# Third column block of an expert product: its last plain products stand among the slices of the seven products, e2 is converted later and in three parts, and the last expert's rows get four buffers

## The chip, the cores and the metric

One core of one Trainium2 chip runs the whole program as one launch. The metric is device time in microseconds (us), the median of the runs shown. One further execution was taken by the hardware profiler; all rows below are of that execution, and a time such as 953.37 is counted from the first instruction of its span.

Engines: PE is TensorE (PEld its weight loads), DVE is VectorE, ACT is ScalarE, POOL is GpSimd, and SP is the engine whose queue issues the plain DMA transfers.

## The reference: what is computed

```python
def reference(**kwargs):
    attn_out = _attn_ref(q, k, v, proj)          # 2 x 8 heads, 768 x 64, masked by hash buckets
    x = attn_out.transpose(0, 2, 1, 3).reshape(B * S, H * D)      # 1536 x 512
    x = ((x @ w1) * (x @ w2) @ w3) @ w_out                        # 512 -> 1024 -> 1024 -> 512
    p = domain_probs / (domain_probs.sum(-1, keepdims=True) + 1e-09)
    out = np.zeros((N, D), dtype=np.float32)
    for e in range(4):
        h = np.maximum(x @ e1[e], 0.0)                            # 1536 x 1024
        out += p[:, e:e + 1] * (h @ e2[e])                        # 1536 x 512
    return out
```

The change touches only the last loop, the four experts (from about 476 us to the end), and mostly `h @ e2[e]`.

## The kernel before, in words

Every float32 operand is split into a high part (made by ACT) and a low part (made by DVE, the difference), and a product is three TensorE passes: high x high, high x low, low x high.

An expert `e` has two stages. The 1536 token rows are three blocks of 512.

**Up stage** (`fp_products`, four steps `fp` = 0 to 3). `x @ e1[e]` is made by seven products instead of eight (Strassen's scheme); `CHAIN` gives their order 1, 2, 6, 5, 7, 4, 3. Each has a part M (512 columns, the first two token blocks) and a part N (256 columns, the third). N gives the third block's rows, kept in `row_y`: four rows of `xa` and two buffers `m_t`.

**Down stage.** For the first two token blocks `h @ e2[e]` is again seven products, in the order 1, 4, 6, 2, 5, 7, 3. Each is cut into four slices (`slice_mm`; slice `p.s` is product p, slice s), each of 12 matmuls of 256 columns into the banks `u_ps`: products 1, 6, 5, 3 into banks 1 and 3 (`YB2`), products 4, 2, 7 into banks 0 and 2 (`WB2`). Product 6 continues in the banks where 1 stood. For the third block the product is plain: eight pieces `y_down(e, 0)` to `y_down(e, 7)`, here O0 to O7, each 12 matmuls of 512 columns into the four banks `o_ps`. In the kernel before O0 to O3 stand in the up stage (behind product 7 of steps 1, 2, 3 and at the end of step 3), and O4 to O7 each stand ahead of one slice of product 1: O4, 1.0, O5, 1.1, O6, 1.2, O7, 1.3, then 4.0 to 4.3, 6.0 and so on.

Operands of the slices:
- Left: a slice's rows are split into one of three buffers `hl` (ACT, then DVE) just ahead of it. Products 6, 5, 7 and 3 read sums. One is made by POOL (`sums_a`); the others are made by accumulating DMA transfers that POOL issues (`added`): those of product 6 are `sums_b`'s `(s, e, 2, s)`. One may go out only when slice `4.s` has been split, since it overwrites what that slice reads.
- Right: e2 comes into `ro` (two halves of 512 columns per `fp`, `load_o`) and is split into ten units of `ring`; POOL makes four sums per `fp` out of `ro` (`t`, L897). The plain product O(2fp+h) uses unit 4h+fp and unit 8+h; units 8 and 9 are reused by each `fp`. `prep_b` writes the sums into units given by `UNITS` when the units are free.

Results: `gather` (DVE, L1065) adds each bank's half into `xa` and, for the last expert, stores it. The third block's rows go through `third` (L1205): load the rows from `out` into the one buffer `xo`, multiply and add o_ps on DVE, store them back; four times per expert, d = 0 to 3, each waiting for the store before. For expert 0 there is nothing to load.

The order on each engine is set by a planner (`emit_all`): every operation has an engine, a planned duration, dependencies and a due time (`clock[0]` counts planned PE time; Q = 2600 ns), and the planner writes the operations into each engine's in-order queue. On the chip an engine then waits at the head of its queue. The planner charges a plain DMA 700 to 800 ns on SP and 1900 ns until it has landed, and an accumulating DMA 1000 ns on POOL and 2200 ns more.

```python
LAT["SP"] = {"PE": 1900, "ACT": 1900, "DVE": 1900, "POOL": 1900, "SP": 1900, "NONE": 0}
for s in range(4):                 # down stage of an expert, before
    y_down(e, 4 + s)
    slice_mm(e, 1, s, free_)
last_o[0] = [third(e, d) for d in range(4)]
```

The functions that the diff touches, with the line numbers of the profile:

Of the kernel before, what the change touches and what calls it, by code (L numbers as in the profile page):

```python
# [85 lines left out]
def tile_lsh_attention_moe(ctx, tc, qk, v, projc, w1, w2, w3T, w_out, dp, e1, e2, out):  # L86
# [789 lines left out]
    def load_o(e, fp):  # L876
        name = ("O", e, fp)
        T = clock[0]
        for h in range(2):
# [15 lines left out]
        for m, x, y, need_ in ((1, quad_(fp, 0, 1), quad_(fp, 0, 0), []), (3, quad_(fp, 1, 1), quad_(fp, 0, 1), []),  # L895
                               (2, quad_(fp, 1, 1), quad_(fp, 0, 0), [("td", e - 1, 6, fp // 2), ("xd", 7, 0), ("xd", 7, 1)]), (4, quad_(fp, 1, 0), b_sum(2, fp), [])):
            op(("t", e, fp, m), "POOL", 700, lambda m=m, x=x, y=y: nc.gpsimd.tensor_tensor(out=b_sum(m, fp)(), in0=x(), in1=y(), op=ALU.subtract),  # L897
               [("dc", name), ("dd", name), ("dl", name, 0), ("dl", name, 1)] + need_ + [("t", e, fp, k) for k in {1: (), 3: (1,), 2: (1,), 4: (2,)}[m]], T + Q)
# [296 lines left out]
    def third(e, d):  # L1195
# [5 lines left out]
        free_ = [("st3", i - 1)] if i else []  # L1201
        T = clock[0] + 15 * Q
        if e:
            op(("l3", i), "SP", 800, lambda: nc.sync.dma_start(out=xo[0], in_=rows), free_ + [("st3", i - 4)], T - 10 * Q)
            op(("ox3", i), "DVE", 650, lambda: nc.vector.scalar_tensor_tensor(  # L1205
                out=xo[0], in0=o_ps[d], scalar=p, in1=xo[0], op0=ALU.mult, op1=ALU.add), src + [("l3", i)], T)
        else:
            op(("ox3", i), "DVE", 650, lambda: nc.vector.tensor_scalar(out=xo[0], in0=o_ps[d], scalar1=p, scalar2=None, op0=ALU.mult),
               src + free_, T)
        op(("st3", i), "SP", 800, lambda: nc.sync.dma_start(out=rows, in_=xo[0]), [("ox3", i)], T)  # L1210
# [4 lines left out]
    UNITS = {1: (0, 1, 2, 3), 4: (0, 1, 8, 9), 6: (2, 3, 0, 1), 2: (4, 5, 6, 7), 5: (8, 9, 2, 3), 7: (0, 1, 4, 5), 3: (6, 7, 8, 9)}  # L1215
# [172 lines left out]
```

## Time and profile before

| what | value |
|---|---|
| median of 3 runs | 976.85 us (975.31 to 977.16) |
| the profiled execution, its own time | 977.87 us |
| its span, first to last instruction | 976.1 us |
| PE busy | 959.2 us, 98% of the span |
| DVE, ACT, POOL busy | 729.5, 574.5, 319.2 us |
| mean granted TensorE clock | 0.997 |

The profiled execution is 1.77 us longer than its span and 1.02 us longer than the median. PE is busy nearly all the time, so what is left to win or lose lies in the places where PE's timeline shows a wait, and in how long PE's work itself takes at the granted clock.

### The profile page before, as it was taken

To read this page: it belongs to the slowest core of one execution; us is meant where nothing else is said; L and a number is where in the kernel's file an instruction comes from. 1 tells how busy PE (TensorE), PEld (TensorE's weight loads), DVE (VectorE), ACT (ScalarE), POOL (GpSimd) and SP (SyncE) were. 2 spreads that over 40 slices of the span, in tenths; PEclk is the share of its full clock that TensorE was granted. 3 is DMA by queue.
4 is the path that set the end of the run, shared out by engine and by line. 5 is a ranking of instruction groups with operands and counts; after the bars stand their busy time and mean duration, and the time that the engine had idled before them with its cause. 6 is when DMAs were issued, how large, how long until landed. Compare 5 with 4: busy or idle time off the path is not lost. (4 is left out here: it accounts for less than half of the span.)

```text
span 976.1 us, 15888 instructions
## 1 busy us (share of the span) xinstructions
PE 959.2 (98%) x5803; PEld 852.0 (87%) x5803; DVE 729.5 (75%) x1403; ACT 574.5 (59%) x1078; POOL 319.2 (33%) x372
## 2 busy tenths in 40 slices
PE   8999999999999999999999999999999999999997
PEld 6989899998888888888788899888998889988887
DVE  6999999998699965955765687556875568754477
ACT  5989989888534322444665554655546555465452
POOL 6888778876100000000102341023410234102340
PEclk9999999999999999999999999999999999999999
DMA  6755444330144421400311083110841108410074
GB/s 165 188 128 129 107 115 112 96 96 12 55 130 130 128 88 44 129 22 1 109 33 33 22 157 114 33 33 22 165 138 33 33 22 167 136 34 11 1 161 131
DMA packets 54110, 84.54 MB, mean 87 GB/s; under 512 B 7016, under 2 KB 28840, under 8 KB 54032
## 3 DMA queue, kind: packets, MB, share of 16 engines
q1 hardware_dynamic: 46976, 70.94, 24.8%
q0 software_dynamic: 6912, 12.59, 7.2%
q8 instruction: 45, 0.74, 0.3%
q14 instruction: 33, 0.27, 0.1%
q10 hardware_dynamic: 144, 0.01, 0.0%
HBM read 50.36 MB, written 6.29 MB: 58 GB/s over the span
## 5 line engine op out<-in xcount | busy, mean ns | idle before, releaser
L176 PE MATMUL u_ps<-ring,hl 128*128 128x256 f32 x1344 | 169.1, 285 | 4.5 <-DVE hl L185 3.7
L176 PEld LDWEIGHTS u_ps<-ring,hl 128*128 128x128 f32 x1344 | 165.7, 193 | 8.8 <-DVE hl L185 6.0
L897 POOL TENSOR_TENSOR ro<-ro 128x256 f32<-128x256 f32 x32 | 28.0, 875 | 279.7 <-DVE ring L185 278.4
L176 PE MATMUL u_ps<-xh,slot 128*128 128x512 f32 (+1 forms) x576 | 114.4, 355 | 0.0
L176 PEld LDWEIGHTS u_ps<-xh,slot 128*128 128x128 f32 x576 | 95.5, 189 | 16.0 <-DVE xh L185 0.4
L494 ACT ACTIVATE e<-e,sm 128x768 f32<-128x768 f32 x96 | 89.3, 932 | 8.0 <-DVE e L491 7.1
L176 PE MATMUL u_ps<-xh,slotl 128*128 128x256 f32 (+1 forms) x456 | 90.5, 346 | 1.5 <-DVE xa L1055 1.5
L176 PE MATMUL o_ps<-ring,hl 128*128 128x512 f32 x384 | 91.9, 390 | 0.0
L491 DVE TENSOR_SCALAR_CACHE_REDUCE e<-s_ps 128x768 f32<-128x768 f32 x96 | 89.9, 948 | 2.3 <-PE t_ps L539 1.4
L176 PEld LDWEIGHTS o_ps<-ring,hl 128*128 128x128 f32 x384 | 71.3, 188 | 14.4
L176 PEld LDWEIGHTS u_ps<-xh,slotl 128*128 128x128 f32 x456 | 72.7, 189 | 12.7 <-DVE xa L1055 1.9
L176 PE MATMUL u_ps<-slot,slotl 128*128 128x512 f32 (+1 forms) x384 | 72.9, 338 | 0.0
L504 POOL TENSOR_SCALAR e<-e,sm 128x768 f32<-128x768 f32 x72 | 67.2, 940 | 11.6 <-DVE sm L509 6.2
L185 DVE TENSOR_TENSOR ring<-ro,ring 128x512 fp32r<-128x512 f32 x48 | 36.5, 759 | 42.0 <-ACT ring L182 40.5
L176 PEld LDWEIGHTS u_ps<-slot,slotl 128*128 128x128 f32 x384 | 59.0, 190 | 8.0
L176 PE MATMUL pv_ps<-etx,vv 128*128 128x256 f32 x384 | 58.2, 290 | 0.1
L1047 ACT ACTIVATE hl<-gl 128x512 fp32r<-128x512 f32 x52 | 32.9, 633 | 42.1 <-PE u_ps L176 18.9
L176 PE MATMUL s_ps<-ka,hh 128*128 128x512 f32 x192 | 53.1, 358 | 2.1 <-DVE e L491 1.7
L176 PEld LDWEIGHTS pv_ps<-etx,vv 128*128 128x128 f32 x384 | 49.8, 189 | 1.9 <-DVE xa L567 0.8
L176 PE MATMUL s_ps<-kb,ll 76*128 76x512 f32 x192 | 49.8, 341 | 0.5 <-DMA kb<-bt 0.5
L1065 DVE SCALAR_TENSOR_TENSOR xa<-u_ps,prob,xa 128x256 f32<-128x256 f32 x112 | 49.4, 482 | 0.9 <-PE u_ps L176 0.9
L176 PE MATMUL u_ps<-xh,slotm 128*128 128x512 f32 x216 | 49.9, 389 | 0.0
(209 smaller groups left out, 2049.2 us busy)
## 6 DMA issues: line engine op xcount, KB each, us to landing
wraw<-in_w SPq DMA_DIRECT2D x16, 512.0 KB
wraw<-in_w3T SPq DMA_DIRECT2D x16, 512.0 KB
wraw<-in_e SPq DMA_DIRECT2D x32, 256.0 KB
ro<-in_e SPq DMA_DIRECT2D x32, 256.0 KB
r<-in_qk SPq DMA_DIRECT2D x15, 384.0 KB
gl<-gl POOLq DMA_DIRECT2D x20, 256.0 KB, 4.5
wraw<-in_w_out SPq DMA_DIRECT2D x8, 512.0 KB
out<-xo SPq DMA_DIRECT2D x16, 256.0 KB
```

Of the source, the lines that this page charges most:

```text
L176: nc.tensor.matmul(out=o, lhsT=l, rhs=r, start=start, stop=stop, skip_group_check=chained)
L185: nc.vector.tensor_tensor(out=dst, in0=ps, in1=f(hi), op=ALU.subtract)
L491: op(("mx", u, t), "DVE", 873, lambda ps=ps, m=m, e=e: nc.vector.tensor_scalar(out=cols(e), in0=row(ps), scalar1=THR, scalar2=None, op0=AL ...
L494: op(("ex", u, t), "ACT", 921, lambda e=e, m=m, rs=rs: nc.scalar.activation(out=e, in_=e, func=AF.Exp, scale=-1.0, bias=m, accum_out=rs), ...
L504: return "POOL", 872, lambda: nc.gpsimd.tensor_scalar(out=e, in0=e, scalar1=r[:, t:t + 1], scalar2=1.0, op0=ALU.mult, op1=ALU.mult)
L897: op(("t", e, fp, m), "POOL", 700, lambda m=m, x=x, y=y: nc.gpsimd.tensor_tensor(out=b_sum(m, fp)(), in0=x(), in1=y(), op=ALU.subtract), [ ...
L1047: op(("gh", n), "ACT", 600, lambda: nc.scalar.activation(out=hi(), in_=src(), func=AF.Relu if relu else AF.Copy, scale=sign), after, T)
L1065: nc.vector.scalar_tensor_tensor(out=xa[:, t, w], in0=src(), scalar=p, in1=xa[:, t, w], op0=ALU.mult, op1=ALU.add)
```

## The change: what it does

1. The plain products move: O0 behind product 7 of step 1, O1 behind product 7 and O2 behind product 3 of step 2, O3 behind product 7 of step 3; then O4 ahead of slice 1.0, O5 ahead of 1.1, O6 ahead of 1.3 and O7 ahead of 6.0 (`BEFORE`). `third` is now called after O7.
2. `load_o` converts an `fp` of e2 in three parts (a left half for each h, and both right halves, units 8 and 9, together) and begins only when PE has done the first product of that step, M part (`GATE`); for expert 0, step 0, the third product. POOL's sums follow the part that each needs.
3. The units of `ring` for products 4, 6, 5, 7 and 3 are dealt anew, so that product 4 no longer uses units 8 and 9.
4. In the last expert the four `third` rows use four buffers: the halves of `raws[0]`, `xo` and `m_t[1]` (`third_buf`), with due times earlier than before.
5. Planner's numbers: an accumulating transfer is charged 3500 ns on a lane per slice index instead of 2200; POOL's sums 840 and 1050 instead of 700; gathers 393 instead of 380; step 1 of expert 0's e1 conversion is due 3 Q later.

```diff
+    for i in range(4):
+        LAT[f"Q{i}"] = dict.fromkeys(LAT["SP"], 0)
...
     def load_u(e, fp, after, z_after):
-        T = clock[0] + (16 * Q if e and fp == 1 else 0)
+        T = clock[0] + ((16 if e else 3) * Q if fp == 1 else 0)
...
+    def GATE(e, fp):
+        return ("M", e, fp, 1 if e or fp else 3)
...
     def load_o(e, fp):
...
-            op(("dh", name, h), "ACT", 600, lambda units=units, src=src: hi_of(units(0), src()),
-               [("dl", name, h)] + unit_free[u] + unit_free[v], T)
-            op(key, "DVE", 620, lambda units=units, src=src: lo_of(units(1), src(), units(0)), [("dh", name, h)], T)
-            unit_free[u], unit_free[v] = None, [("O", e, 2, 2 * fp + h)]
+            op(("dh", name, h), "ACT", 340, lambda unit_at=unit_at, src=src: hi_of(unit_at(0), src()), [("dl", name, h), gate] + unit_free[u], T)
+            op(key, "DVE", 350, lambda unit_at=unit_at, src=src: lo_of(unit_at(1), src(), unit_at(0)), [("dh", name, h)], T)
+            unit_free[u] = None
+        op(("dh", name, 2), "ACT", 600, lambda: hi_of(ring[0][:, 8:10, 0], ro[0][:, fp, :, 256:512]),
+           [("dl", name, 0), ("dl", name, 1), gate] + unit_free[8] + unit_free[9], T)
+        op(("de", name), "DVE", 620, lambda: lo_of(ring[0][:, 8:10, 1], ro[0][:, fp, :, 256:512], ring[0][:, 8:10, 0]), [("dh", name, 2)], T)
...
     def third(e, d):
-        free_ = [("st3", i - 1)] if i else []
-        T = clock[0] + 15 * Q
+        final = e == NE - 1
+        free_ = ([raw_free[0], raw_free[0], [("st3", i - 3)], t_free[5]][d] if final else [("st3", i - 1)] if i else [])
+        T = clock[0] + (4 if final else 15) * Q
...
-    UNITS = {1: (0, 1, 2, 3), 4: (0, 1, 8, 9), 6: (2, 3, 0, 1), 2: (4, 5, 6, 7), 5: (8, 9, 2, 3), 7: (0, 1, 4, 5), 3: (6, 7, 8, 9)}
+    UNITS = {1: (0, 1, 2, 3), 4: (0, 1, 2, 3), 6: (0, 1, 8, 9), 2: (4, 5, 6, 7), 5: (2, 3, 0, 1), 7: (8, 9, 4, 5), 3: (6, 7, 2, 3)}
...
-        op(("s", e, m, s), "NONE", 2200, lambda: None, [("sq", e, m, s)], T)
+        op(("s", e, m, s), f"Q{s}", 3500, lambda: None, [("sq", e, m, s)], T)
...
+    BEFORE = ((1, 0), (1, 1), (1, 3), (6, 0))
...
+    def third_buf(e, d):
+        if e < NE - 1:
+            return xo[0]
+        return (raws[0][:, 0:512], raws[0][:, 512:1024], xo[0], m_t[1])[d]
+
     for e in range(NE):
         for fp in range(4):
             fill = {}
             if fp:
-                fill[7] = (lambda: y_down(e, fp - 1),)
-            if fp == 3:
-                fill[3] = (lambda: y_down(e, 3),)
+                fill[7] = (lambda: y_down(e, (0, 0, 1, 3)[fp]),)
+            if fp == 2:
+                fill[3] = (lambda: y_down(e, 2),)
...
+        downs = iter(range(4, KF))
         for s in range(4):
-            y_down(e, 4 + s)
+            if (1, s) in BEFORE:
+                y_down(e, next(downs))
             slice_mm(e, 1, s, free_)
-        last_o[0] = [third(e, d) for d in range(4)]
...
             for s in range(4):
+                if (p, s) in BEFORE:
+                    y_down(e, next(downs))
+                    if (p, s) == BEFORE[-1]:
+                        last_o[0] = [third(e, d) for d in range(4)]
                 slice_mm(e, p, s, free_)
```

**PE, last expert, from product 4 into product 6.** A slice is two rows (one per bank); `u_ps0` and `u_ps2` are product 4's banks, `u_ps1` and `u_ps3` product 6's. Before:

```order
L176 MATMUL u_ps0_3015<-ring_4484,hl2_3000 128x256 x6
L176 MATMUL u_ps2_3017<-ring_4484,hl2_3000 128x256 x6
L176 MATMUL u_ps0_3015<-ring_4484,hl0_2998 128x256 x6
L176 MATMUL u_ps2_3017<-ring_4484,hl0_2998 128x256 x6
L176 MATMUL u_ps1_3016<-ring_4484,hl1_2999 128x256 x6
L176 MATMUL u_ps3_3018<-ring_4484,hl1_2999 128x256 x6
```

After, the same place (slices 4.2, 4.3, then O7 in the four banks `o_ps`, then 6.0):

```order
L176 MATMUL u_ps0_3015<-ring_4484,hl1_2999 128x256 x6
L176 MATMUL u_ps2_3017<-ring_4484,hl1_2999 128x256 x6
L176 MATMUL u_ps0_3015<-ring_4484,hl2_3000 128x256 x6
L176 MATMUL u_ps2_3017<-ring_4484,hl2_3000 128x256 x6
L176 MATMUL o_ps0_3019<-ring_4484,hl0_2998 128x512 x3
L176 MATMUL o_ps1_3020<-ring_4484,hl0_2998 128x512 x3
L176 MATMUL o_ps2_3021<-ring_4484,hl0_2998 128x512 x3
L176 MATMUL o_ps3_3022<-ring_4484,hl0_2998 128x512 x3
L176 MATMUL u_ps1_3016<-ring_4484,hl1_2999 128x256 x6
L176 MATMUL u_ps3_3018<-ring_4484,hl1_2999 128x256 x6
```

One plain product now stands between 4.3 and 6.0, and none between 1.2 and 4.0 but O6. The same holds in the other three experts.

**DVE, last expert, around the third row of the third block (o_ps2).** Before:

```order
L1049 SCALAR_TENSOR_TENSOR hl2_3000<-gl0_2996,hl2_3000 128x512
L1065 SCALAR_TENSOR_TENSOR xa_72<-u_ps3_3018,prob_59,xa_72 128x256
L1205 SCALAR_TENSOR_TENSOR xo0_3004<-o_ps2_3021,prob_59,xo0_3004 128x512
L1267 SCALAR_TENSOR_TENSOR ring_4484<-ro_4483,ring_4484 128x2x256
L185 TENSOR_TENSOR hl0_2998<-cbuf_71,hl0_2998 128x512
L185 TENSOR_TENSOR hl1_2999<-g0_68,hl1_2999 128x512
```

After, all four rows of the third block (`wraw0` is `raws[0]`), each out of a buffer of its own:

```order
L1223 SCALAR_TENSOR_TENSOR wraw0_69<-o_ps0_3019,prob_59,wraw0_69 128x512
L1223 SCALAR_TENSOR_TENSOR wraw0_69<-o_ps1_3020,prob_59,wraw0_69 128x512
L185 TENSOR_TENSOR ring_4484<-wraw1_70,ring_4484 128x2x256
L185 TENSOR_TENSOR hl0_2998<-gl1_2997,hl0_2998 128x512
L185 TENSOR_TENSOR hl1_2999<-gl1_2997,hl1_2999 128x512
L1223 SCALAR_TENSOR_TENSOR xo0_3004<-o_ps2_3021,prob_59,xo0_3004 128x512
L185 TENSOR_TENSOR ring_4484<-ro_4483,ring_4484 128x2x256
L1063 SCALAR_TENSOR_TENSOR hl2_3000<-cbuf_71,hl2_3000 128x512
L1223 SCALAR_TENSOR_TENSOR m1_3003<-o_ps3_3022,prob_59,m1_3003 128x512
```

They moved forward to the slices of product 6 and the start of product 2. In experts 1 and 2 the four stand further apart and all use `xo`; the third (d = 2) stands between the splits for slices 7.0 and 7.1. In expert 0 the second (d = 1) stands three rows behind the first, just ahead of the split for slice 2.0.

**DVE, first expert's first step, up to the addition that frees the bank of N's product 5** (`xa<-xa,u_ps`). The `ring` rows are e2's conversion, the `xh` rows left operands of products 1, 2 and 5. Before:

```order
L857 TENSOR_TENSOR wraw_69<-wraw_69,zf 128x2x128 x2
L185 TENSOR_TENSOR ring<-ro,ring 128x2x256
L185 TENSOR_TENSOR xh_2993<-gl_2997,xh_2993 128x2x256
L185 TENSOR_TENSOR ring<-ro,ring 128x2x256
L185 TENSOR_TENSOR xh_2993<-gl_2997,xh_2993 128x2x256
L185 TENSOR_TENSOR xh_2993<-gl_2996,xh_2993 128x2x256
L993 TENSOR_TENSOR gl_2996<-gl_2997,gl_2996 128x512
L993 TENSOR_TENSOR gl_2996<-gl_2997 128x512
L993 TENSOR_TENSOR gl_2996<-gl_2997,gl_2996 128x512
L1055 TENSOR_TENSOR xa<-xa,u_ps_3018 128x256
```

After:

```order
L861 TENSOR_TENSOR wraw_69<-wraw_69,zf 128x2x128 x2
L185 TENSOR_TENSOR xh_2993<-gl_2997,xh_2993 128x2x256 x2
L185 TENSOR_TENSOR xh_2993<-gl_2996,xh_2993 128x2x256
L1007 TENSOR_TENSOR gl_2996<-gl_2997,gl_2996 128x512
L1007 TENSOR_TENSOR gl_2996<-gl_2997 128x512
L1069 TENSOR_TENSOR cbuf<-cbuf,u_ps_3016 128x512
L1069 TENSOR_TENSOR xa<-xa,u_ps_3018 128x256
```

The two conversions leave this place; in three parts they now stand behind the addition that follows product 3 (seven rows further down), and POOL's sums follow them. One subtraction has moved behind `xa`, one addition ahead of it.

## Rows read from the trace of the kernel before

**Rows 1.** The page, part 1: busy time of each engine, its share, instructions.

```profile
PE 959.2 (98%) x5803; PEld 852.0 (87%) x5803; DVE 729.5 (75%) x1403; ACT 574.5 (59%) x1078; POOL 319.2 (33%) x372
```

**Rows 2.** Groups by line and shape, PE, 478 to 973: busy, mean ns | idle before.

```profile
L176 PE MATMUL u_ps<-ring,hl 128*128 128x256 f32 x1344 | 169.1, 285 | 4.5 <-DVE hl L185 3.7 <-DVE hl L1049 0.5
...
L176 PE MATMUL u_ps<-xh,slotl 128*128 128x256 f32 x192 | 28.2, 283 | 1.5 <-DVE xa L1055 1.5
```

**Rows 3.** PE's timeline: start, length, instruction, [idle before <- releaser].

```profile
488.05 2.37 PE L176 MATMUL u_ps<-xh,slotl 128*128 128x256 f32 x12 [1.52 <-DVE xa L1055]
...
818.77 3.47 PE L176 MATMUL u_ps<-ring,hl 128*128 128x256 f32 x24 [0.22 <-DVE hl L185]
822.41 23.05 PE L176 MATMUL u_ps<-ring,hl 128*128 128x256 f32 x190 [0.17 <-DVE hl L1049]
...
927.46 2.91 PE L176 MATMUL o_ps<-ring,hl 128*128 128x512 f32 x12
930.21 9.26 PE L176 MATMUL u_ps<-ring,hl 128*128 128x256 f32 x74
939.70 1.69 PE L176 MATMUL u_ps<-ring,hl 128*128 128x256 f32 x12 [0.23 <-DVE hl L185]
941.69 1.70 PE L176 MATMUL u_ps<-ring,hl 128*128 128x256 f32 x12 [0.29 <-DVE hl L185]
943.73 7.45 PE L176 MATMUL u_ps<-ring,hl 128*128 128x256 f32 x60 [0.35 <-DVE hl L185]
953.37 18.71 PE L176 MATMUL u_ps<-ring,hl 128*128 128x256 f32 x142 [2.19 <-DVE hl L185]
```

**Rows 4.** Stretches of 1 us: length, busy of PE, PEld, DVE, ACT, POOL, granted clock.

```profile
954.00:955.00 1.00, 1.00 (x6) 1.00 (x6) 1.00 (x3) 0.00 (x0) 0.00 (x0) 0.50 0.00 0
...
956.00:957.00 1.00, 1.00 (x8) 1.00 (x7) 0.94 (x3) 0.32 (x1) 0.00 (x0) 0.68 0.74 201
```

**Rows 5.** DVE's timeline, experts 2 and 3: rows of `third`, and three gathers.

```profile
820.41 0.75 DVE L1205 SCALAR_TENSOR_TENSOR xo<-o_ps,prob,xo 128x512 f32<-128x512 f32 x1
...
827.45 0.75 DVE L1205 SCALAR_TENSOR_TENSOR xo<-o_ps,prob,xo 128x512 f32<-128x512 f32 x1
...
942.33 0.75 DVE L1205 SCALAR_TENSOR_TENSOR xo<-o_ps,prob,xo 128x512 f32<-128x512 f32 x1
...
945.39 1.27 DVE L1065 SCALAR_TENSOR_TENSOR xa<-u_ps,prob,xa 128x256 f32<-128x256 f32 x3
...
951.36 0.75 DVE L1205 SCALAR_TENSOR_TENSOR xo<-o_ps,prob,xo 128x512 f32<-128x512 f32 x1 [2.50 <-DMA xo<-out]
```

**Rows 6.** SP's timeline, the same two experts: issues of stores and loads of `xo`.

```profile
821.18 0.34 SPq L1210 DMA_DIRECT2D out<-xo  x1
823.43 0.33 SPq L1204 DMA_DIRECT2D xo<-out  x1
...
943.11 0.34 SPq L1210 DMA_DIRECT2D out<-xo  x1
947.10 0.33 SPq L1204 DMA_DIRECT2D xo<-out  x1
```

**Rows 7.** ACT's timeline, experts 2 and 3: a split of product 6 each.

```profile
817.36 0.63 ACT L1047 ACTIVATE hl<-gl 128x512 fp32r<-128x512 f32 x1 [1.26 <-DMA gl<-gl]
...
938.28 0.63 ACT L1047 ACTIVATE hl<-gl 128x512 fp32r<-128x512 f32 x1 [2.41 <-DMA gl<-gl]
```

**Rows 8.** DVE's timeline, first step of expert 0.

```profile
481.19 0.69 DVE L185 TENSOR_TENSOR xh<-gl,xh 128x512 fp32r<-128x512 f32 x1
481.79 1.23 DVE L185 TENSOR_TENSOR ring<-ro,ring 128x512 fp32r<-128x512 f32 x1
482.94 2.37 DVE L185 TENSOR_TENSOR xh<-gl,xh 128x512 fp32r<-128x512 f32 x2
...
487.59 0.41 DVE L1055 TENSOR_TENSOR xa<-xa,u_ps 128x256 f32<-128x256 f32 x1
```

**Rows 9.** POOL's timeline at the same place: the first two sums of e2.

```profile
481.50 2.12 POOL L897 TENSOR_TENSOR ro<-ro 128x256 f32<-128x256 f32 x2 [223.29 <-DVE ring L185]
```

More of the change, by code (lines that the diff above doesn't have):

```diff
@@ L255, in tile_lsh_attention_moe @@
     }
+    for i in range(4):
+        LAT[f"Q{i}"] = dict.fromkeys(LAT["SP"], 0)
+        for e in LAT:
+            LAT[e][f"Q{i}"] = 0
     ops = []
@@ L877, in load_o @@
         name = ("O", e, fp)
+        gate = GATE(e, fp)
         T = clock[0]
@@ L881, in load_o, with unit_at @@
                 out=ro[0][:, fp, h], in_=e2[e][(2 * fp + h) * 128:(2 * fp + h + 1) * 128, :]), ro_free[fp], T - 1.5 * P)
-            u, v = 4 * h + fp, 8 + h
+            u = 4 * h + fp
             key = ("dd" if h else "dc", name)
-            def units(b, u=u, v=v):
-                return ring[0][:, u:v + 1:v - u, b]
+            def unit_at(b, u=u):
+                return ring[0][:, u, b]
             def src(h=h):
-                return ro[0][:, fp, h].rearrange("p (u c) -> p u c", u=2)
@@ L891, in load_o @@
-            op(("dh", name, h), "ACT", 600, lambda units=units, src=src: hi_of(units(0), src()),
-               [("dl", name, h)] + unit_free[u] + unit_free[v], T)
-            op(key, "DVE", 620, lambda units=units, src=src: lo_of(units(1), src(), units(0)), [("dh", name, h)], T)
-            unit_free[u], unit_free[v] = None, [("O", e, 2, 2 * fp + h)]
[L895 to L898, printed above, removed]
+                return ro[0][:, fp, h, 0:256]
@@ new lines, in load_o @@
+        for h in range(2):
+            unit_free[8 + h] = [("O", e, 2, 2 * fp + h)]
+        for m, x, y, need_ in ((1, quad_(fp, 0, 1), quad_(fp, 0, 0), [("dc", name)]),
+                               (2, quad_(fp, 1, 1), quad_(fp, 0, 0), [("t", e, fp, 1), ("td", e - 1, 6, fp // 2), ("xd", 7, 0), ("xd", 7, 1)]),
+                               (4, quad_(fp, 1, 0), b_sum(2, fp), [("dd", name), ("t", e, fp, 2)]),
+                               (3, quad_(fp, 1, 1), quad_(fp, 0, 1), [("t", e, fp, 1), ("de", name)])):
+            op(("t", e, fp, m), "POOL", 1050 if m == 2 else 840, lambda m=m, x=x, y=y: nc.gpsimd.tensor_tensor(out=b_sum(m, fp)(), in0=x(), in1=y(), op=ALU.subtract),
+               [("dl", name, 0), ("dl", name, 1)] + need_, T + Q)
@@ L1065, in go @@
                 nc.vector.scalar_tensor_tensor(out=xa[:, t, w], in0=src(), scalar=p, in1=xa[:, t, w], op0=ALU.mult, op1=ALU.add)
-        op(key, "DVE", 650 if w.stop - w.start == 512 else 380, go, after + region.get((t, w.start), []) + [("gdone", 1 + t // KF, t % KF)], clock[0] + later * Q)
+        op(key, "DVE", 650 if w.stop - w.start == 512 else 393, go, after + region.get((t, w.start), []) + [("gdone", 1 + t // KF, t % KF)], clock[0] + later * Q)
         region[t, w.start] = [key]
@@ L1200, in third, with x @@
         src = [("O", e, 2, KF - 1)]
[L1201 to L1202 removed]
+        final = e == NE - 1
+        free_ = ([raw_free[0], raw_free[0], [("st3", i - 3)], t_free[5]][d] if final else [("st3", i - 1)] if i else [])
+        T = clock[0] + (4 if final else 15) * Q
+        def x():
+            return third_buf(e, d)
         if e:
[L1204 removed]
+            op(("l3", i), "SP", 800, lambda: nc.sync.dma_start(out=x(), in_=rows), free_ + [("st3", i - 4)], T - 10 * Q)
             op(("ox3", i), "DVE", 650, lambda: nc.vector.scalar_tensor_tensor(
[L1206 removed]
+                out=x(), in0=o_ps[d], scalar=p, in1=x(), op0=ALU.mult, op1=ALU.add), src + [("l3", i)], T)
         else:
[L1208 removed]
+            op(("ox3", i), "DVE", 650, lambda: nc.vector.tensor_scalar(out=x(), in0=o_ps[d], scalar1=p, scalar2=None, op0=ALU.mult),
                src + free_, T)
[L1210 removed]
+        op(("st3", i), "SP", 800, lambda: nc.sync.dma_start(out=rows, in_=x()), [("ox3", i)], T)
         return ("ox3", i)
     YB2, WB2 = (1, 3), (0, 2)
[L1215 removed]
+    UNITS = {1: (0, 1, 2, 3), 4: (0, 1, 2, 3), 6: (0, 1, 8, 9), 2: (4, 5, 6, 7), 5: (2, 3, 0, 1), 7: (8, 9, 4, 5), 3: (6, 7, 2, 3)}
     A_OF = {1: (0, 0), 4: (1, 1), 6: (1, 1), 2: (0, 1), 5: (0, 0), 7: (1, 0), 3: (0, 1)}
```

4 lines of the change are left out of this document (2 added, 2 removed).

## The prediction, made before the changed kernel was run

> **What bounds the kernel now.** Read the busy shares first: PE is busy 98% of the span, DVE 75%, the others less [rows 1]. So the time is PE's work, plus PE's waits, plus what a lower clock adds. Next come the waits, by group of instructions, over the four experts [rows 2]: the slices of the down stage waited 4.5 us in all, for `hl` (3.7 us for the plain split, 0.5 us for the scaled one), and one group of the up stage 1.5 us. The plain products do not stand there with a wait. Then PE's timeline shows where [rows 3]:
>
> - 488.05: part N of product 5 in expert 0's first step waited 1.52 us for DVE's addition that frees its bank.
> - 818.77 and 822.41: in expert 2 slice 6.2 waited 0.22 and slice 2.0 0.17 us. Experts 0 and 1 show the same pair, so three pairs of some 0.39 us, 1.2 us in all.
> - 939.70, 941.69, 943.73: in the last expert 6.1, 6.2 and 6.3 waited 0.23 + 0.29 + 0.35 = 0.87 us.
> - 953.37: 2.19 us.
>
> Who was late? For product 6 it is the accumulating transfer: ACT idled for it 1.26 us ahead of the split of 817.36 and 2.41 us ahead of that of 938.28 [rows 7]. For 953.37 it is the load of `xo`: DVE stood 2.50 us at the head of its queue, with the splits for PE behind it [rows 5]. That wait has a second price. After it the granted clock is 0.50 and still 0.68 two microseconds later [rows 4], the lower level of 1.2 GHz where it had been 2.4. In expert 2, 190 matmuls took 23.05 us, 0.1213 us each; the 142 behind 953.37 took 18.71 us, where 142 x 0.1213 = 17.2 [rows 3]. The clock cost 1.5 us. At 488.05, behind 1.52 us, nothing like it is seen.
>
> So there are 1.52 + 1.17 + 0.87 + 2.19 + 1.5 = 7.25 us to be had in the experts, and the same PE instructions run before and after.
>
> **What each part of the change is worth.**
>
> *The order of the plain products.* A plain product takes 930.21 - 927.46 = 2.75 us and a slice 23.05 / 16 = 1.44 us [rows 3]. With O7 between 4.3 and 6.0, product 6 has 2.75 us more behind product 4, from whose splits the transfers start. The lateness to cover is the waits themselves, 0.22 us in experts 0 to 2, and up to 0.87 us together in the last. 2.75 covers each with over 1.5 us to spare; 2.0's 0.17 us came from the splits of product 6 bunched in DVE's queue, and goes with them. Gain 1.17 + 0.87 = 2.04 us.
>
> *Four buffers.* All four loads of the last expert can go out once the up stage and expert 2's last store are through, more than 15 us ahead of their use, so the 2.50 us on DVE go: gain 2.19 + 1.5 = 3.7 us. What moves instead: d = 0 and 1 stand back to back behind O7, 2 x 0.75 us, then product 6's second unit conversion and the split of 6.2, 2 x 0.69 [rows 8]: 2.88 us at most against 2 slices = 2.88. Durations overlap a little at their ends (two of the conversions in rows 8 begin 0.60 us apart), so I take nothing, and 0.2 us as the upper end.
>
> *e2 converted later.* Two conversions leave DVE's chain ahead of the late addition. The first shows no stretch; from 481.50 POOL makes its sums [rows 9], and beside them a conversion takes 1.23 us instead of 0.69, and two `xh` rows 2.37 us [rows 8]. Taking out two rows at 0.6 us and the stretch of these three (0.54 and 2.37 - 1.29 = 1.08) gives 2.8 us, against a wait of 1.52; the addition then ends by 485.2, ahead of the end of product 4's matmuls at 486.53 (488.05 - 1.52). One addition now stands ahead of it (0.6 us) and one subtraction has left. Gain 1.52 us. The conversions and sums now lie beside the next step's work, where DVE has two-input rows as well; the four sums can stretch it by up to 4 x 0.54 us. PE has some 6 us of matmuls queued there, so I charge 0.2, between 0 and 1.5. The three parts add one row on each of DVE and ACT per step, hidden: DVE is busy 75%.
>
> *Fewer plain products ahead of product 4.* Its units 2 and 3 come free at the end of 1.3, and 4.2 needs them two slices later, 2.88 us. ACT takes 0.63 us [rows 7], DVE first makes three gathers in 1.27 us [rows 5], then converts in 0.69: 1.96 us, and the split of 4.2 behind it ends at 2.65. The margin is 0.2 us. If a POOL sum stretches one row by 0.54 us, PE waits 0.3 us. Bounds 0 and 0.3 in each expert, taken 0.1: 0.4 us in all.
>
> *`third` later, in experts 0 to 2.* Here `xo` stays one buffer, and the four turns run among products 6, 2, 5 and 7. The trace gives two prices for a turn. In expert 2 the store was issued at 821.18, the load at 823.43 (it waits until the store has landed: 2.25 us), and d = 2 ran 7.04 us behind d = 1 without a wait. In the last expert, beside more accumulating transfers, store to load took 3.99 us and the turn 9.03 us [rows 5, 6].
>   - Expert 0 has no load. d = 1 stands only three rows behind d = 0. Counted from O7's end, d = 0 ends at 0.75, so its store has landed at 3.0 to 4.8. Behind d = 1 stand a conversion and the split of 2.0: 0.66 + 0.60 + 0.69 = 1.95 us to be done by 4 slices = 5.76, so d = 1 must start by 3.8. PE waits 0 to 1.0 us; I take 0.4.
>   - Experts 1 and 2: d = 1 comes behind the split of 2.3, at about 8.9, when its row is there in both cases (9.03 behind 0, limit 9.5). d = 2 stands ahead of the split of 7.1: its row is there at 8.9 + 7.04 = 15.9 or + 9.03 = 17.9, and it must start by 13 slices less 0.66 + 0.69, 17.4. PE waits 0 to 0.5 us in each; I take 0.25, so 0.5 for both.
>
> By the Trainium skill, DMA: Bandwidth & Descriptors, section Anatomy of one DMA, a transfer costs about 2.0 us plus its bytes over 436 GB/s, an estimate of 2.6 us for 256 KB. By it the sum would be 0.9 us better, since neither turn would be late; the trace's 3.99 us store contradicts it where transfers crowd.
>
> *The rest.* The planner's durations run on no engine; they only set the order. The end of the chain, gathers and stores of product 3, is unchanged.
>
> **Sum.** Gains 2.04 + 3.7 + 1.52 = 7.25 us, new waits 0.2 + 0.4 + 0.4 + 0.5 = 1.5: 5.75 us. The profiled execution lies 1.77 us over its span, and 1.02 us over the median of 976.85; I take the difference off both alike: span 970.35, its own time 972.1, and 971.1 us for the median. With all new waits at their upper ends (1.5 + 0.2 + 1.2 + 1.0 + 1.0 = 4.9) it is 974.5, with none 969.6.
>
> **The rivals.**
>
> *A: e2's work is only moved.* POOL's sums and DVE's two-input rows meet in every step, now ahead of slices that stand without a plain product between them (1.1 and 1.2). For it speaks that DVE is stretched whenever they meet; against it that the stretch is 0.54 us a row and the rows are spread. If expert 0's wait stays (1.52) and each expert gains one of 0.5 us, 2 us: 971.1 + 3.5 = 974.6.
> The Trainium skill, SBUF — State Buffer, section Who interferes with whom, says that a DVE row with two SBUF inputs and a GpSimd row that reads SBUF exclude each other fully. By that rule each such meeting costs a whole POOL row, 1.06 us here; the trace shows 0.54, half of it. With a whole row in each expert A would stand at 971.1 + 1.5 + 4 = 976.6, no change.
>
> *B: the turns of `xo` decide; slower.* If in experts 1 and 2 store and load crowd with the accumulating transfers of product 3's left operand so that a turn takes 11 us or more, d = 2 comes at 19.9, PE waits 2.5 us, and behind such a wait the clock falls as at 953.37, another 1.5. That is 4 us in each, 8 in both, and expert 0 can add 1.0 at the upper store time: 971.1 + 8 = 979. It decides from a turn of some 10.5 us: below, PE waits under 2 us. Against it: 9.03 us, with 2.5 of waiting in it, is the longest turn seen here.
>
> *C: product 6 stays late.* The transfers go through one in-order queue on POOL, and one that serves product 5 stands among those of product 6. If it holds up the rest by as much as the order gives, 2.04 us of gain are lost: 973.1. Against it: it needs only the first transfer to have landed, which starts some 8 us ahead of 6.0.
>
> *D: the conversions of units come late.* With 0.3 us in each expert at 4.2 and another 0.4 at 6.2, where ACT must wait for O7 to free units 8 and 9: 4 x 0.7 = 2.8, less the 0.4 taken: 973.5; with the clock's price or a stretched row more, 975 to 977, no change.
>
> **How the numbers follow.** A difference under 0.2% (2 us) can't be told from no change. Chances: forecast 0.62, A 0.10, B 0.06, C 0.10, D 0.12. Of the forecast and of C nearly all is faster by over 0.2% (below 974.9), of A half, of D half: 0.62 + 0.10 + 0.05 + 0.06 = 0.83. Within 0.2%: 0.12, from A, D and a tenth of B's lighter cases; slower 0.05, from B. The forecast's own range is 969.6 to 973.5. To leave out no more than 2 in 10 it goes up to 975.0 for A, C and D, and down to 969.0, since the runs before differ by up to 1.9 us.
>
> **What the profile of the changed kernel would show.** Right: no wait at part N of product 5 in expert 0; no wait of ACT for `gl<-gl` ahead of product 6; no DVE wait for a load in the last expert, and a granted clock of 1.00 to the end; PE's waits at slices below 2 us in all where 4.5 stood. A shows as DVE rows near 1.2 us ahead of 1.2 to 4.0 with PE waiting; B as DVE waiting for `xo<-out` in experts 1 and 2, or for the store in expert 0; C as ACT still waiting for `gl<-gl`; D as PE waiting at 4.2 and 6.2. The prediction is wrong if a wait of about 2 us or more appears in experts 0 to 2, for then the clock's price comes with it.

## The result, and the profile after

The changed kernel took **966.98 us** (median of 4 runs, 966.70 to 968.08); the kernel before, on the same chip, 976.08 us (4 runs, 974.59 to 977.16). The ratio is 0.991, 95% interval 0.9893 to 0.9927: 9.1 us less, where 5.75 were forecast, and below the stated range. The profiled execution after took 966.7 us, its span is 964.9 us: 11.2 us less than the span before.

Page of the kernel after, part 1 (as [rows 1]):

```profile
PE 953.5 (99%) x5803; PEld 849.8 (88%) x5803; DVE 726.5 (75%) x1419; ACT 572.2 (59%) x1094; POOL 315.7 (33%) x372
```

Groups by line and shape on PE in the experts, after (as [rows 2]):

```profile
L176 PE MATMUL u_ps<-ring,hl 128*128 128x256 f32 x1344 | 163.8, 283 | 0.0
...
L176 PE MATMUL u_ps<-xh,slotl 128*128 128x256 f32 x192 | 28.1, 283 | 0.2 <-DVE xa L1069 0.2
```

The slices wait 0.0 us where they waited 4.5, and the other group 0.2 where it waited 1.5. But the same 1344 matmuls are also *busy* 5.3 us less (163.8 against 169.1). 5.3 + 4.5 + 1.3 = 11.1, the whole gain. Of the 5.3, 1.6 is the low clock of before [rows 4]; the other 3.7 us stand in rows that ran at the upper clock both times. So a third of the gain was hidden in what the matmul rows call busy.

PE's timeline after, last expert from slice 1.3 on, and the one wait left in the experts (as [rows 3]):

```profile
499.29 0.98 PE L176 MATMUL u_ps<-xh,slotl 128*128 128x256 f32 x6 [0.20 <-DVE xa L1069]
...
921.97 7.36 PE L176 MATMUL u_ps<-ring,hl 128*128 128x256 f32 x60
929.16 2.91 PE L176 MATMUL o_ps<-ring,hl 128*128 128x512 f32 x12
931.91 28.95 PE L176 MATMUL u_ps<-ring,hl 128*128 128x256 f32 x240
```

The last 240 matmuls run in one row without a wait, 28.95 / 240 = 0.1206 us each. One microsecond of that stretch (as [rows 4]) has the clock at its upper level:

```profile
954.00:955.00 1.00, 1.00 (x11) 1.00 (x10) 0.75 (x2) 0.21 (x1) 0.00 (x0) 1.00 0.00 0
```

ACT's timeline after, splits of 6.1, 6.2 and 6.3 in the last expert (as [rows 7], whose second line is 6.1): no wait for `gl<-gl`, ACT now waits for PE.

```profile
929.24 0.64 ACT L1061 ACTIVATE hl<-gl 128x512 fp32r<-128x512 f32 x1 [0.81 <-PE u_ps L176]
...
932.65 0.62 ACT L1061 ACTIVATE hl<-gl 128x512 fp32r<-128x512 f32 x1
933.42 0.63 ACT L1061 ACTIVATE hl<-gl 128x512 fp32r<-128x512 f32 x1 [0.16 <-PE u_ps L176]
```

DVE's timeline after, expert 0's first step (as [rows 8]):

```profile
481.30 1.89 DVE L185 TENSOR_TENSOR xh<-gl,xh 128x512 fp32r<-128x512 f32 x3
...
484.90 0.42 DVE L1069 TENSOR_TENSOR xa<-xa,u_ps 128x256 f32<-128x256 f32 x1
...
491.21 2.67 DVE L185 TENSOR_TENSOR ring<-ro,ring 128x512 fp32r<-128x512 f32 x3
...
496.49 1.28 DVE L185 TENSOR_TENSOR slotl<-wraw,slotl 128x256 fp32r<-128x256 f32 x1
...
498.83 0.41 DVE L1069 TENSOR_TENSOR xa<-xa,u_ps 128x256 f32<-128x256 f32 x1
```

The three `xh` rows take 1.89 us where two took 2.37, and the addition that was late at 487.59 begins at 484.90. The conversions and the stretched rows stand behind it, beside POOL's work: an `slotl` row, 0.43 us long at 487.79, takes 1.28 at 496.49, and the addition of 498.83 makes PE wait 0.20. POOL's row at that place is a sum of a left operand, which now comes behind e2's sums:

```profile
496.19 1.29 POOL L1247 TENSOR_TENSOR cbuf<-cbuf 128x512 f32<-128x512 f32 x1
```

DVE's rows of `third` after, experts 0, 1 and 3 (as [rows 5]):

```profile
572.61 0.75 DVE L1226 TENSOR_SCALAR xo<-o_ps,prob 128x512 f32<-128x512 f32 x1 [0.59 <-DMA out<-xo]
...
690.01 0.74 DVE L1223 SCALAR_TENSOR_TENSOR xo<-o_ps,prob,xo 128x512 f32<-128x512 f32 x1
699.11 0.75 DVE L1223 SCALAR_TENSOR_TENSOR xo<-o_ps,prob,xo 128x512 f32<-128x512 f32 x1
706.71 0.75 DVE L1223 SCALAR_TENSOR_TENSOR xo<-o_ps,prob,xo 128x512 f32<-128x512 f32 x1
...
931.85 1.40 DVE L1223 SCALAR_TENSOR_TENSOR wraw<-o_ps,prob,wraw 128x512 f32<-128x512 f32 x2
```

In expert 0 DVE waits 0.59 us for the store of d = 0. In expert 1, d = 1 comes 9.10 us and d = 2 16.70 us behind d = 0, and DVE waits for neither. PE waits for none of these rows.

### The profile page after: what moved, and what is told of

It is laid out like the page before. It is cut to its first block, busy times and chain, and to the rows that moved or that the text cites. A ratio compares the mean times of both kernels' runs of the same rounds, so it can differ in the third digit from the quotient of the medians.

```text
span 964.9 us, 15892 instructions
## 1 busy us (share of the span) xinstructions
PE 953.5 (99%) x5803; PEld 849.8 (88%) x5803; DVE 726.5 (75%) x1419; ACT 572.2 (59%) x1094; POOL 315.7 (33%) x372
## 4 chain that ended last, share of the span: by engine, by line
PE 89%; DVE 7%; ACT 3%; issue 1%; DMA 0%; SPq 0%; DVEq 0%; ACTq 0%
PE u_ps L176 59%; PE o_ps L176 14%; PE s_ps L176 6%; PE pv_ps L176 5%; DVE e L495 2%; PE t_y L176 2%; PE t_ps L543 2%; PE t_x L543 2%; DVE etx L551 1%; ACT e L498 1%; PE t_y L543 1%; DVE ety L551 1%; ACT etx L549 1%; ACT ety L549 0%; DMA r<-in_qk 0%
## 5 line engine op out<-in xcount | busy, mean ns | idle before, releaser
L176 PEld LDWEIGHTS u_ps<-ring,hl 128*128 128x128 f32 x1344 | 163.4, 192 | 1.2
L176 PE MATMUL u_ps<-ring,hl 128*128 128x256 f32 x1344 | 163.8, 283 | 0.0
L185 DVE TENSOR_TENSOR ring<-ro,ring 128x256 fp32r<-128x256 f32 (+1 forms) x64 | 37.6, 610 | 23.5 <-ACT ring L182 21.0
L176 PEld LDWEIGHTS u_ps<-xh,slotm 128*128 128x128 f32 x216 | 40.6, 188 | 8.4
```

The costliest lines, as they stand in the source:

```text
L176: nc.tensor.matmul(out=o, lhsT=l, rhs=r, start=start, stop=stop, skip_group_check=chained)
L185: nc.vector.tensor_tensor(out=dst, in0=ps, in1=f(hi), op=ALU.subtract)
```

## What the weight loads show

The matmul rows of before hid something, so I went to the rows of PE's weight loads. In a slice `hl` is the weight: a late `hl` stops the load, and only through it the matmul. Weight loads of before with a wait, start, length, [idle before <- releaser]; the first three are expert 0's first step, then slices 6.2, 6.3 and 2.0 of expert 2, then the last expert:

```profile
481.93 0.66 PEld L176 LDWEIGHTS u_ps<-xh,slot 128*128 128x128 f32 x5 [0.20 <-DVE xh L185]
484.22 0.66 PEld L176 LDWEIGHTS u_ps<-xh,slot 128*128 128x128 f32 x5 [0.24 <-DVE xh L185]
488.05 1.93 PEld L176 LDWEIGHTS u_ps<-xh,slotl 128*128 128x128 f32 x12 [1.95 <-DVE xa L1055]
...
818.77 1.48 PEld L176 LDWEIGHTS u_ps<-ring,hl 128*128 128x128 f32 x12 [0.43 <-DVE hl L185]
820.55 1.49 PEld L176 LDWEIGHTS u_ps<-ring,hl 128*128 128x128 f32 x12 [0.29 <-DVE hl L185]
822.41 22.84 PEld L176 LDWEIGHTS u_ps<-ring,hl 128*128 128x128 f32 x190 [0.37 <-DVE hl L1049]
938.97 0.30 PEld L176 LDWEIGHTS u_ps<-ring,hl 128*128 128x128 f32 x2 [0.17 <-ACT hl L1047]
939.70 1.49 PEld L176 LDWEIGHTS u_ps<-ring,hl 128*128 128x128 f32 x12 [0.43 <-DVE hl L185]
941.68 1.50 PEld L176 LDWEIGHTS u_ps<-ring,hl 128*128 128x128 f32 x12 [0.50 <-DVE hl L185]
943.73 7.24 PEld L176 LDWEIGHTS u_ps<-ring,hl 128*128 128x128 f32 x60 [0.55 <-DVE hl L185]
953.36 18.51 PEld L176 LDWEIGHTS u_ps<-ring,hl 128*128 128x128 f32 x142 [2.39 <-DVE hl L185]
```

Against [rows 3], each wait of a slice is 0.20 to 0.21 us longer here (0.43 for 0.22, 0.37 for 0.17, 2.39 for 2.19), that of 488.05 0.43 longer, and seven waits of 0.17 to 0.29 us do not stand among the matmul rows at all (820.55, for one). The sum from 474 us on is 9.9 us in 18 waits, where the matmul rows show 5.7 in 11. That the matmul rows show less fits with their ends being modelled. The Trainium skill, Perfetto Trace Analysis, section Tensor Engine Instruction (MATMUL, LD_WEIGHTS), says the same of the chip's profiler: a TensorE end time is computed from the instruction's size, not observed.

After the change only two are left from 474 us on, 0.67 us in all, both in expert 0's first step:

```profile
496.02 0.77 PEld L176 LDWEIGHTS u_ps<-xh,slot 128*128 128x128 f32 x6 [0.27 <-DVE xa L1069]
...
499.29 0.77 PEld L176 LDWEIGHTS u_ps<-xh,slotl 128*128 128x128 f32 x6 [0.40 <-DVE xa L1069]
```

What a wait costs can also be read without either engine's idle time, from the starts of the matmul rows. Where nothing waits, a slice takes 1.44 us from start to start: the 240 matmuls above, less the 0.28 us of the last one, give 28.67 / 239 x 12. In [rows 3] it is 1.99 us from 939.70 to 941.69 and 2.04 from there to 943.73, so the waits at 941.69 and 943.73 cost 0.55 and 0.60 us. The weight loads show 0.50 and 0.55 of that, the matmul rows 0.29 and 0.35.

**Theory 1**: the gain is removed waits, at the price that the weight-load rows show, plus the clock. **Theory 2** (rival): they cost what the matmul rows show, and the rest comes from elsewhere in the change. **Theory 3**: the four buffers only move the late wait to another releaser. **Theory 4**: the later place of `third`, not the four buffers, removes the wait for `xo`.

## The experiments

Ratios are to the kernel before on the same chip, with their 95% intervals.

**The four buffers alone.** Kernel before plus:

```diff
-        free_ = [("st3", i - 1)] if i else []
-        T = clock[0] + 15 * Q
+        final = e == NE - 1
+        free_ = ([raw_free[0], raw_free[0], [("st3", i - 3)], t_free[5]][d] if final else [("st3", i - 1)] if i else [])
+        T = clock[0] + (4 if final else 15) * Q
```

(and `third_buf`, as in the change).

> The kernel before with one part alone: the last expert's four rows of the third block get four buffers, and their due times are earlier. Theory 1 (a wait costs what the weight-load rows of PE show, plus the clock behind it): the 2.39 us in front of 953.36 and the 1.5 us of lower clock go, the 1.65 us of product 6 in the last expert stay: about 972.2 us. Theory 2 (a wait costs what the matmul rows show, the rest of the 9 us comes from elsewhere): 2.19 + 1.5 less, about 972.4, so this run does not tell 1 from 2. Theory 3 (the late load only hides a lateness of the accumulating transfers behind it): the wait stays at the same place with another releaser, 975 to 976.

974.64 us, ratio 0.9993 (0.998 to 1.0006): no gain that can be told, where 3.9 us were expected. Its weight loads in the last expert:

```profile
939.33 0.30 PEld L176 LDWEIGHTS u_ps<-ring,hl 128*128 128x128 f32 x2 [0.90 <-ACT hl L1047]
940.06 1.50 PEld L176 LDWEIGHTS u_ps<-ring,hl 128*128 128x128 f32 x12 [0.43 <-DVE hl L185]
942.49 5.81 PEld L176 LDWEIGHTS u_ps<-ring,hl 128*128 128x128 f32 x48 [0.94 <-DVE hl L185]
948.50 19.97 PEld L176 LDWEIGHTS u_ps<-ring,hl 128*128 128x128 f32 x166 [0.19 <-DVE hl L1049]
```

The wait for `xo` is gone and the clock stays up, but product 6 now waits 2.27 us (0.90 + 0.43 + 0.94) instead of 1.65, and slice 2.2 behind it 0.19: theory 3 in part. The 12 runs lie within 1.5 us, while 23 of the kernel before spread over 6.2 us (971.94 to 978.14). What that spread is, the last two runs below tell.

**The later start alone.** Kernel before plus the gate on e2's conversion:

```diff
-               [("dl", name, h)] + unit_free[u] + unit_free[v], T)
+               [("dl", name, h), ("M", e, fp, 1 if e or fp else 3)] + unit_free[u] + unit_free[v], T)
```

> The kernel before with one part alone: e2's conversion (still in two parts) begins only when PE has done the first product of the step, M part, third product for expert 0, step 0. Theory 1: the waits in front of the weight loads of 481.93, 484.22 and 488.05 (0.20 + 0.24 + 1.95 = 2.39 us) go: about 973.7 us. Theory 2: 1.52 us go, 974.6. Rival A of the prediction (the work is only moved): other waits come, 975.5 to 977.

973.61 us, ratio 0.9981 (0.9967 to 0.9996). The three waits of the first step are gone, no new ones come, and the waits of product 6 and of `xo` (2.17 us) stay. Against the 975.37 us of the kernel before in the same runs the gain is 1.8 us, between the 2.4 of theory 1 and the 1.5 of theory 2, and the interval excludes neither.

**One buffer in the last expert.** The changed kernel with:

```diff
-        final = e == NE - 1
+        final = False
...
-        if e < NE - 1:
+        if e < NE:
             return xo[0]
```

> The changed kernel with the last expert's rows back in the one buffer, as in experts 0 to 2. If the four buffers are what removes the late load of xo (the prediction's term of 3.7 us), about 970.7 us, with DVE waiting for xo and PE behind it. Theory 4: standing later, among products 6, 2, 5 and 7, the rows of the last expert turn around as in experts 1 and 2, where nothing waits: 967.0 to 967.5, no wait on PE.

966.58 us, ratio 0.9917 (0.9899 to 0.9936), like the changed kernel's 0.991: theory 4 holds, in so far as the later place is enough without the buffers. DVE's rows of `third`, last expert, in this kernel:

```profile
930.96 0.75 DVE L1223 SCALAR_TENSOR_TENSOR xo<-o_ps,prob,xo 128x512 f32<-128x512 f32 x1
940.06 0.74 DVE L1223 SCALAR_TENSOR_TENSOR xo<-o_ps,prob,xo 128x512 f32<-128x512 f32 x1
948.03 0.75 DVE L1223 SCALAR_TENSOR_TENSOR xo<-o_ps,prob,xo 128x512 f32<-128x512 f32 x1 [0.46 <-DMA xo<-out]
953.97 0.74 DVE L1223 SCALAR_TENSOR_TENSOR xo<-o_ps,prob,xo 128x512 f32<-128x512 f32 x1
```

Turns of 9.10, 7.97 and 5.94 us; DVE waits 0.46 us in all and PE not at all, since the splits behind these rows are not yet due.

**O7 earlier.** The changed kernel with:

```diff
-    BEFORE = ((1, 0), (1, 1), (1, 3), (6, 0))
+    BEFORE = ((1, 0), (1, 1), (1, 2), (1, 3))
```

The first kernel of the two leaves out `third` altogether (its call stands in the second loop, which no longer comes to the last entry).

> The changed kernel with O6 ahead of slice 1.2 and O7 ahead of 1.3 again, so that no plain product stands between 4.3 and 6.0. Theory 1: product 6's waits come back at what the weight loads showed before, 1.05, 1.33, 1.09 and 1.65 us in the four experts, 5.1 us: about 972.1 us. Theory 2: what the matmul rows showed, 2.04 us: 969.0. If other parts (fewer plain products ahead of product 4, the lanes of the planner) removed the waits of product 6: 967.0, and ACT waits for gl before 6.0 without a wait on PE.

968.93 us, ratio 0.9942 (0.9922 to 0.9963). Product 6 waits once in each expert, 0.30, 0.43, 0.43 and 0.37 us, 1.5 us in all: far less than the 5.1 foretold. The time is the one that theory 2 gave (969.0), but by chance: the matmul rows show only 0.6 us of these waits, while the span is 1.6 us longer than the changed kernel's.

The second kernel calls `third` behind the first loop, so nothing is left out:

> The changed kernel with O6 ahead of slice 1.2 and O7 ahead of 1.3 again, the rows of the third block kept (the run before left them out). If the earlier rows of the third block add nothing, as the run before: waits of 0.3 to 0.43 us in front of a weight load of product 6 in each expert, 1.5 us, 968.5 us. If these rows stand in the way of product 6's splits as before the change: its three waits an expert come back, 1.05 to 1.65 us each, 5.1 us in all, 972 us.

971.69 us, ratio 0.9971 (0.9957 to 0.9986). Expert 1, DVE and then the weight load:

```profile
697.64 0.75 DVE L1223 SCALAR_TENSOR_TENSOR xo<-o_ps,prob,xo 128x512 f32<-128x512 f32 x1 [2.34 <-DMA xo<-out]
```

```profile
699.04 4.37 PEld L176 LDWEIGHTS u_ps<-ring,hl 128*128 128x128 f32 x36 [1.70 <-DVE hl L1063]
```

So the place of O7 ahead of 6.0 is worth 4.9 us (5.56 us of waits here, less the 0.67 that the changed kernel has too) in two ways: 2.1 us at product 6 (0.32 + 0.31 + 0.43 + 0.41 + 0.62), and 2.8 us for `xo` in experts 1 and 2 (1.70 + 0.20 + 0.69 + 0.21). The second is rival B's mechanism, which the changed kernel escapes by the later place. The 972 us that the expectation gave were met by luck: it put all 5.1 us at product 6, where only 2.1 came, and the rows of `xo` made up the time. So the place of O7 does not explain all that product 6 gained; the other 3.0 us must go with other parts of the change, and no run shows which.

**No gate.** The changed kernel with:

```diff
-        return ("M", e, fp, 1 if e or fp else 3)
+        return ("se",)
```

> The changed kernel with e2's conversion, in three parts, free to begin as soon as its operands are there. If the later start is what removes the waits of expert 0's first step: 2.39 us in front of three weight loads come back, 969.4 us, and the later steps show nothing new. If the three parts and the new planned durations suffice: 967.0.

972.51 us, ratio 0.9973 (0.996 to 0.9986): 5.5 us more than the changed kernel, not 2.4. Weight loads in the first step of expert 0:

```profile
487.62 1.22 PEld L176 LDWEIGHTS u_ps<-xh,slotl 128*128 128x128 f32 x6 [2.41 <-DVE cbuf L1069]
489.78 0.66 PEld L176 LDWEIGHTS u_ps<-slot,slotl 128*128 128x128 f32 x5 [0.71 <-DVE slot L185]
496.94 0.85 PEld L176 LDWEIGHTS u_ps<-y,zs 128*128 128x128 f32 x5 [2.29 <-DVE y L185]
```

With 0.72 us at 483.40 these are 6.1 us of waits in this step, where the kernel before had 2.4; two later steps wait 0.86 us more, and the lower clock behind the last wait costs 1.7. Without the gate the conversions of later steps crowd into it: nine of DVE's `ring<-ro` rows, three per step, lie between 479 and 494 us.

**Old planner's numbers** (2200 on no lane, 700, 380, and the old due time, as on the minus side of the change):

> The changed kernel with the planner's old numbers (accumulating transfer 2200 on no lane, POOL's sums 700, gathers 380, step 1 of expert 0's e1 conversion due as before). If the numbers matter as little as the prediction took them to: 966.5 to 967.5 and no wait in the experts. If the planner needs the longer transfer to keep the splits of product 6 out of the head of ACT's and DVE's queues: part of product 6's waits is back, 968 to 971.

966.23 us, ratio 0.9907 (0.9892 to 0.9923). One wait of 0.74 us at 499; the numbers do not matter.

**The order** (no gate, one buffer, old numbers; the units dealt anew and the conversion in three parts stay):

> The changed kernel without the later start, without the four buffers and with the planner's old numbers: what is left is the order of the plain products, the units dealt anew and the conversion in three parts. Theory 1 with theory 4 (the order frees product 6 and lets the rows of the third block turn around among later products): only expert 0's 2.39 us are left, 969.4 us. If the other parts are needed: 971 to 974, with waits at product 6 or for xo in the last expert.

972.07 us, ratio 0.9968 (0.9952 to 0.9984). All six waits, 5.58 us, lie between 482 and 499; from there to the end no weight load waits. The order of the plain products, with these two parts, frees the whole down stage, the last expert with its single `xo` included; expert 0's first step costs more than foretold, as without the gate above.

**Order and gate** (one buffer, old numbers; again with the units and the three parts):

> The changed kernel without the four buffers and with the planner's old numbers: the order of the plain products, the units, the conversion in three parts and its later start are left. If these parts make all of the gain: 966 to 967.5 us, no wait in front of a weight load but one of under 1 us at 499, and none in the last expert. If the planner's numbers or the four buffers matter once the other is gone: 969 to 971.

966.67 us, ratio 0.9929 (0.9912 to 0.9946), two waits of 0.74 and 0.23 us, the second in the last expert, where none was expected. These parts make the whole gain; the buffers and the numbers add nothing that can be measured. The units and the three parts were not tried by themselves.

**Two `hl` instead of three, for many waits.** The changed kernel, in the experts with:

```diff
-        return n, ([("hf", n - NHL)] if n >= NHL else sw)
+        b = n % (2 if two[0] else NHL)
+        last = user.get(b)
+        user[b], bufof[n] = n, b
+        return n, (sw if last is None else [("hf", last)])
```

> The changed kernel with two buffers hl instead of three in the experts, so that a slice's rows are split only after the slice two before it has ended, and nearly each of the 112 slices waits a little. Theory 1 (the weight-load rows of PE show what a wait costs): the time grows by 20 to 50 us, and the span less the waits of the weight-load rows in the experts stays at 964 to 966 us (more, if the clock falls). Theory 2 (the matmul rows show it): the span less the waits of the matmul rows stays there; by theory 1 the matmul rows show some 0.2 us less at each wait, 20 us or more in all, so the span less these is above 980.

993.61 us, ratio 1.0206 (1.0185 to 1.0228). Groups in the experts, matmuls and then weight loads:

```profile
L176 PE MATMUL u_ps<-ring,hl 128*128 128x256 f32 x1344 | 176.9, 287 | 17.2 <-DVE hl L185 14.1 <-DVE hl L1068 2.8
...
L176 PEld LDWEIGHTS u_ps<-ring,hl 128*128 128x128 f32 x1344 | 167.2, 191 | 27.5 <-DVE hl L185 21.1 <-DVE hl L1068 4.3
```

There were 42 waits, not 112, and longer ones, so the two theories stand 9 us apart and not 20. The span less the weight loads' waits is 993.9 - 26.1 = 967.8, less the matmul rows' 976.8. Theory 1 comes much nearer, but this is 3 us above the others. Some 2 us of it are the 0.05 us by which, as the starts of the rows showed above, a wait costs more than its weight load shows, 42 times; the rest stays open.

**The kernel before, twice again.**

> The kernel before, profiled again, for its spread (971.5 to 978.1 us in the runs of it so far, where the changed kernel lies within 2.2 us). If the late load of xo in the last expert and the clock behind it make the spread: the wait of 953.37 is shorter in a faster run, by as much as the run is, and the others stay. If not, the waits are the same and the difference lies ahead of the experts.

> The same as the run before it, once more: a second point for the length of the last expert's wait against the time of the run.

975.76 and 973.20 us. The slower one waits 2.20 us for `xo` at 951.19 with the low clock behind it; in the faster one the load of `xo` is late by 0.85 us on DVE, at another turn, and PE shows only this in the last expert:

```profile
942.16 0.30 PEld L176 LDWEIGHTS u_ps<-ring,hl 128*128 128x128 f32 x2 [0.56 <-ACT hl L1047]
942.89 24.32 PEld L176 LDWEIGHTS u_ps<-ring,hl 128*128 128x128 f32 x202 [0.43 <-DVE hl L185]
```

So of three profiled executions of the kernel before two have the wait for `xo` and its clock (3.9 to 4.0 us together) and one has not: it is a large part of their spread, and [rows 3 to 5] show an execution that had it, at 977.87 us near the top of the spread.

**All kernels together.** Waits are summed over the timeline from 474 us on; the clock's cost is the busy share of each microsecond times the clock missing in it, up to the last 9 us (for order_only, whose record stands at 0.95 throughout at an unchanged pace of matmuls, relative to 0.95). Where nothing else differs, the last column must agree.

| kernel | span | waits, matmul rows | waits, weight loads | low clock | span less matmul waits and clock | span less weight-load waits and clock |
|---|---|---|---|---|---|---|
| before | 976.1 | 5.7 | 9.9 | 1.6 | 968.8 | 964.6 |
| before_again | 974.0 | 4.9 | 8.2 | 1.7 | 967.4 | 964.1 |
| before_once_more | 971.4 | 3.1 | 6.6 | 0 | 968.4 | 964.8 |
| b_four | 972.7 | 4.3 | 8.4 | 0 | 968.4 | 964.3 |
| b_gate | 973.1 | 3.8 | 7.0 | 1.7 | 967.6 | 964.4 |
| order_only | 971.3 | 3.5 | 5.6 | 1.6 | 966.2 | 964.1 |
| a_no_gate | 971.3 | 5.3 | 7.0 | 1.7 | 964.3 | 962.6 |
| a_o7_at_13 | 969.8 | 3.0 | 5.6 | 0 | 966.8 | 964.2 |
| a_o7_early | 966.5 | 0.8 | 2.2 | 0 | 965.7 | 964.3 |
| a_old_numbers | 965.0 | 0.5 | 0.7 | 0 | 964.5 | 964.3 |
| order_gate | 964.6 | 0.5 | 1.0 | 0 | 964.1 | 963.6 |
| a_one_xo | 964.2 | 0.2 | 0.7 | 0 | 964.0 | 963.5 |
| after | 964.9 | 0.2 | 0.7 | 0 | 964.7 | 964.2 |
| a_two_hl | 993.9 | 17.1 | 26.1 | 0 | 976.8 | 967.8 |

Without the last row, 962.6 to 964.8 by the weight loads, 964.0 to 968.8 by the matmul rows, and by the latter, order_only apart, the more waits a kernel has in the slices, the higher. Why a_no_gate lies lowest, 1.6 us under the changed kernel, stays open. Theory 2 falls: no part of the change made the slices themselves faster.

## Why the prediction missed

- **Product 6, gain 2.04 us: the step that failed most.** The mechanism was right (ACT no longer waits for `gl<-gl`), the size was not, and the place of O7 is not all of it. "The lateness to cover is the waits themselves, 0.22 us in experts 0 to 2, and up to 0.87 us together in the last" read PE's matmul rows. The weight loads show 1.05, 1.33, 1.09 and 1.65 us, 5.1 in all. With O7 back ahead of 1.3, ACT waits for `gl<-gl` again (5.8 us in six waits), but only 2.1 us return at product 6 (a_o7_at_13).
- **e2 converted later, gain 1.52 us.** Right, and again read too small: 0.20 + 0.24 + 1.95 = 2.39 us. The addition was foretold to end by 485.2 and ended at 485.3. The charge for the later place (0.2 of 0 to 1.5) was 0.67: the weight loads at 496.02 and 499.29 wait 0.27 and 0.40.
- **Four buffers, gain 3.7 us.** For the profiled execution the size was right: 2.39 of waiting and 1.57 of clock. The cause was given to the wrong part: the step costed the later `third` only as a risk in experts 0 to 2, and did not ask what it does in the last. There the later place removes the wait without the buffers (a_one_xo); the buffers alone remove it too, but make product 6 later and bring nothing that can be told (b_four).
- **New waits, charged 1.5 us.** Product 4's units and the turns of `xo` made PE wait nowhere. Expert 0's d = 1 began 3.52 us behind d = 0, within its limit; d = 2 in expert 1 came 16.70 us behind, within 17.4. In the changed kernel only the 0.67 us above are left.
- **The sum.** 5.1 + 2.4 + 4.0 - 0.7 = 10.8 us against 11.2 of the spans and 5.75 forecast. The missing 5.05 are 3.1 (product 6), 0.9 (first step), 0.3 (`xo`) and 0.8 (new waits).
- **Profiled execution and median.** "I take the difference off both alike" was wrong for a wait that not every execution has: the profiled one had it, so the gain in medians, 9.1 us, is smaller than the 11.2 of the profiles.
- **The range** put bounds on each new wait and none on the gains, so its low end left out what came.
- **The rivals.** A shows only as the 0.67 us; C and D do not show; B came in a_o7_at_13, with 2.8 us. By the Trainium skill, SBUF — State Buffer, section Who interferes with whom, from which A drew its rule, such DVE and POOL rows exclude each other. The trace is near to that: when the `slotl` row began at 496.49, 0.99 us were left of POOL's row (to 497.48), and it was stretched by 0.85; before the change 0.77 us were left beside the conversion of 481.79 (half of POOL's 2.12 us, from 481.50), and it was stretched by 0.54. In both the price is somewhat under what was left, so the whole POOL row that the prediction took for each meeting was too much.
- **Two smaller slips**, on which nothing rests. The Trainium skill, DMA: Bandwidth & Descriptors, section Anatomy of one DMA, gives the formula that the prediction quotes for transfers issued by GpSimd. The rows of `xo` go through SP's queue. And 190 matmuls are not 16 slices but two matmuls fewer.
